# Block 9's burst of attention, block 10's centring and two last stores moved in a fused attention and feed-forward kernel

## The chip, the cores and the metric

The kernel runs on one core of one Trainium2 chip. The metric is device time in microseconds of one execution. A core has five engines with instruction queues of their own: TensorE (PE; matmuls and transposes, its weight loads are listed as PEld), VectorE (DVE), ScalarE (ACT), GpSimd (POOL) and SyncE (SP, which only issues transfers here). The engines run side by side and wait for one another through semaphores; each does its own instructions in the order in which they stand. Transfers are issued from SyncE, ScalarE and GpSimd.

## The reference

Two stages, one behind the other. The first is attention over a sliding window of 128 positions with a linear distance penalty for each head; the second centres and scales each row, runs two dense layers with a ReLU between them, and adds its input.

```python
# q, k, v: 8 batches x 8 heads x 576 positions x 64
scores = scale * np.matmul(q, k.transpose(0, 1, 3, 2))
bias = slopes[:, None, None] * (-np.abs(rel).astype(np.float32))[None, :, :]
mask = (rel >= 0) & (rel < window)
scores = np.where(mask, scores + bias[None], -1000000000.0)
attn = softmax(scores)                  # written out in the reference
x = matmul(attn, v), heads side by side # 8 x 576 x 512

mu, var = mean and variance of each row of x
xn = (x - mu) / np.sqrt(var + 1e-06) * g_ln
out = x + np.maximum(xn @ w_ch1, 0.0) @ w_ch2   # w_ch1 512 x 2048, w_ch2 2048 x 512
```

Inputs and output are float32; the kernel computes with 16-bit floats and sums in float32.

## The kernel before, in words

**Blocks and groups.** The 4608 rows are handled as 36 blocks of 128 rows, in four pairs of batches with nine blocks each (`order`); the ninth block of a pair takes the last 64 positions of both batches. Blocks are gathered into groups for the dense layers: six groups of two blocks (0 to 11), then six of four (`GROUPS`). Groups from `FAST` (6) on do the second layer in another way, with seven products in place of eight (`fast_mlp2`); the change's first part lies before them, its last in the last of them.

**Attention for one block.** Queries and keys are loaded by GpSimd two blocks at a time and turned (`turn`): for the first three pairs of batches TensorE transposes them (L301) into the two score banks (`ps_sc0`, `ps_sc1`), and VectorE copies one bank out and ScalarE the other (L333, L334). The scores of a block (`attend`, L436) go into the same two banks, half of the heads in each; ScalarE takes the exponential (L445) into `probs`, VectorE multiplies it by the mask and decay (L456), and TensorE multiplies by V (L489) into a bank of the pool `ps_mm`. VectorE divides by the sums (L497, L498), which gives `x`.

**Centring.** From block 8 on, `stats` takes mean and variance of `x` on VectorE (L586, L587) and GpSimd makes the reciprocal root of the variance (L541, L544); `normal` then centres and scales on VectorE (L528, into `xc`), and SyncE transposes the result by a transfer (L536) into the group's tile `xT`.

**Dense layers.** `mlp1` has 16 units: four matmuls each (L730) into a bank of `ps_mm`, and one relu, on ScalarE (L746) or for a few units on VectorE (L738). `mlp2` takes each block of the group through four times four matmuls (L763), and `finish` adds `x` on VectorE (L906) and stores. `ps_mm` has four banks, shared by these layers, the products with V and the second layer's sums; a bank is free again when its reader is done.

**What sets the order.** TensorE, VectorE, ScalarE and SyncE have their order written out. `steps` is a list of small pieces of attention work. For each block n from 8 on it has four kinds, here called by letters: A (products with V of block n and scores of block n+2), B (masks of blocks n+1 and n+2, statistics of n), C (a turn further on, where one is due), D (`normal` of block n). `weave_at` runs the units of a dense layer and, behind the units named in its list of places, takes the next pieces from `steps`. The order of GpSimd's instructions (loads, reciprocal roots) isn't written out: a scheduler places them.

In the kernel before, the pieces near the change stand thus: in `mlp1` of group 3, A of block 9 behind unit 13; in its `mlp2`, B9 behind unit 0, C10 (the turn of block 13) and D9 behind unit 1, A10 behind 3, B10 behind 4, D10 behind 5, A11 behind 6; in `mlp1` of group 4, B11 behind unit 0, C12 (the turn of block 15) behind 4, D11 behind 8, A12 and B12 behind 10.

**The last stores.** In the last group, `fast_mlp2` stores the first two blocks whole and the other two by halves of columns: the high half when its sum is ready, the low half, block by block, behind the last product. `store` writes each block in two transfers and gives them in turn to the queues it is told: SyncE and ScalarE. The sums come from VectorE (L847), the stores stand at L921 (the ninth block of a pair) and L925 (the others).

Of the kernel before, what the change touches and what calls it, by code (L numbers as in the profile page):

```python
# [23 lines left out]
NSLOT = 9  # L24
HALF = P // 2
GROUPS = [2] * 6 + [4] * 6
FAST = 6

NV = 10
BY_DMA_TURN = 3  # L30
# [29 lines left out]
def kernel(  # L60
# [10 lines left out]
    nc = tc.nc  # L71
# [548 lines left out]
    for g, size in enumerate(GROUPS):  # L620
        n = sum(GROUPS[:g])
# [3 lines left out]
    count = len(order)  # L625
# [23 lines left out]
    def masks_of(n, *halves):  # L649
        return [(masks,) + order[n] + halves]  # L650

    def warm_step(n):
        return [[(warm, n)]]


    steps = warm_step(11) + [[(turn_first,)]] + warm_step(3)
# [27 lines left out]
    def turn_at(n):  # L684
        ahead = [m for m in (n + 3, n + 4) if m < count and order[m][1] % 2 == 0]
        return [
            f
            for m in ahead
            if by_dma(order[m][0]) == (m == n + 4)
            for f in turn_step(m, True)  # L690
        ]

    steps.append(turn_at(8))
    for n in range(8, count):
        first_half, second_half = values_steps(n)
        step = first_half + second_half[:1]
        if n + 1 < count and order[n + 1][1] == T:
            step += [(scores_tail, order[n][0])]
        if n + 2 < count:
            step += scores_step(n + 2)  # L700
        steps.append(step)
        steps.append(
            [m for t in (n + 1, n + 2) if t < count for m in masks_of(t)] + [(stats, n)]
        )
        if n + 1 < count:
            steps.append(turn_at(n + 1))
        steps.append([(normal, n)])
    combined = combine_w2()
    done = 0

# [10 lines left out]
    def mlp1(g, on_dve=()):  # L721
# [5 lines left out]
        for u, fb in enumerate(turn_about if g >= FAST else range(NFB)):  # L727
# [21 lines left out]
            yield cols  # L749
            if g >= FAST and u == 10:  # L750
                for i in range(4):
                    combine_hidden(g, 0, i)

    def mlp2(g, parts=((0, NFB),)):

        ht = hidden[g]
        sums = {}
        for first, end in parts:
            for at, (p, blk) in enumerate(members[g]):
                if first == 0:  # L760
                    sums[at] = ps_mm.tile([P, DM], FP32, tag="mm", name="ps_m2")
                for fb in range(first, end):
                    nc.tensor.matmul(  # L763
                        sums[at],
                        ht[:, fb, at * P : (at + 1) * P],
                        w2[:, fb, :],
                        start=(fb == 0),
                        stop=(fb == NFB - 1),
                    )
                    if fb % 4 == 3 and fb < NFB - 1:  # L770
                        yield DM
                if end == NFB:
                    finish(p, blk, sums[at])
                    yield DM
# [25 lines left out]
    def fast_mlp2(g):  # L800

        pairs = len(members[g]) // 2
        n0 = sum(GROUPS[:g])
        outs = [out_pool.tile([P, 2, DM], FP32, tag="o", name="o") for _ in range(2)]

        def rows(i):  # L810
            if pairs == 1:
                return x_pairs[n0 // 2][:, i : i + 1, :], outs[0][:, i : i + 1, :]
            return x_pairs[n0 // 2 + i], outs[i]

        x_bank, z_bank, *others = ring
        use = dict(x=[x_bank] * 2, z=[z_bank] * 2)
        use["y"] = use["w"] = others[:1] * 2
        if g == len(GROUPS) - 1:
            use["w"] = others
        ring[:] = others  # L820
        banks = {
            name: [b.rearrange("p (j d) -> p j d", j=2) for b in bs]
            for name, bs in use.items()
        }

        def product(name, lhs, rhs, first):
            for pair in range(pairs):
                for fb in range(QF):
                    nc.tensor.matmul(  # L829
                        banks[name][pair][:, pair, :],  # L830
                        lhs[:, fb, pair * P : (pair + 1) * P],
                        rhs[:, fb, :],
                        start=(
                            first
                            and fb == 0
                            and (pair == 0 or use[name][0] is not use[name][1])
                        ),
                        stop=(fb == QF - 1),
                        skip_group_check=True,
                    )  # L840
                if pair < pairs - 1:
                    yield DM

        def add(name, i, j, to_x, at=slice(0, pairs)):
            x, o = rows(i)
            cols = slice(j * QD, (j + 1) * QD)
            nc.vector.tensor_tensor(  # L847
                out=o[:, at, cols],
                in0=banks[name][at.start][:, at, :],
                in1=(x if to_x else o)[:, at, cols],  # L850
                op=ALU.add,
            )

        def send(i, ats=range(pairs), cols=slice(0, DM), queues=(nc.sync,)):
            _, o = rows(i)
            for at in ats:
                store(*members[g][i * pairs + at], o[:, at, :], cols, queues)

        a = [[hidden_quarter(g, i, j) for j in range(2)] for i in range(2)]
        s = [hidden_sum(g, i) for i in range(4)]  # L860
        combine_hidden(g, 1, 0)
        combine_hidden(g, 1, 1)
        yield from product("x", a[0][0], quarter(0, 0), True)
        add("x", 0, 0, True)
        combine_hidden(g, 1, 2)
        yield DM
        yield from product("y", a[0][1], quarter(1, 0), True)
        add("y", 0, 0, False)
        combine_hidden(g, 1, 3)
        yield DM  # L870
        yield from product("z", s[0], t1, True)
        add("z", 1, 1, True)
        yield DM
        yield from product("x", s[1], t2, False)
        add("x", 0, 1, True)
        yield DM
        yield from product("z", s[3], quarter(1, 1), False)
        add("z", 0, 1, False)
        send(0, queues=(nc.sync, nc.scalar) if g == len(GROUPS) - 1 else (nc.sync,))
        yield DM  # L880
        yield from product("x", s[2], t3, False)
        add("x", 1, 1, False)
        low, high = slice(0, QD), slice(QD, DM)
        if g == len(GROUPS) - 1:
            send(1, cols=high, queues=(nc.sync, nc.scalar))
        add("x", 1, 0, True)
        if use["w"][0] is use["w"][1]:
            yield DM
            ring[:] = [others[1], z_bank, x_bank, others[0]]
            yield from product("w", a[1][1], t4, True)  # L890
            add("w", 1, 0, False)
            send(1)
            yield DM
        else:
            last = product("w", a[1][1], t4, True)
            yield DM
            for at in range(pairs):
                next(last, None)
                add("w", 1, 0, False, slice(at, at + 1))
                send(1, [at], low, (nc.sync, nc.scalar))  # L900
                yield DM
# [27 lines left out]
    def weave_at(units, *places, also=()):  # L929
        for u, _ in enumerate(units):  # L930
            advance_to(done + places.count(u))
            if u in also:
                next(combined, None)
# [13 lines left out]
    with tc.manual_schedule(engines={engine.PE, engine.SP}):  # L947
        with tc.manual_schedule(engines={engine.Activation, engine.DVE}):
            advance_to(first)
            weave_at(mlp1(0, (0, 1)), 2, 7, 8, 9, 13)  # L950
            weave_at(mlp1(1), 2, 8, 12)
            weave_at(mlp2(0, ((0, 8), (8, 12), (12, NFB))), 0, 1, 3, 4, 4, 5)
            weave_at(mlp2(1), 0, 1, 2, 3, 4, 6, 6)
            weave_at(mlp1(2), 0, 3, 3, 6, 8, 11)
            weave_at(mlp2(2), 0, 2, 4, 6, 7)


            weave_at(mlp1(3, (9, 10, 11)), 8, 8, 12, 13)
            weave_at(mlp2(3), 0, 1, 1, 3, 4, 4, 5, 6)
            weave_at(mlp1(4), 0, 4, 8, 10, 10, 14)  # L960
            weave_at(mlp2(4), 0, 2, 2, 5, 5, 7, also=(1, 4, 6))
            weave_at(mlp1(5), 0, 5, 5, 8, 10, 12, also=(3, 6, 9))
            weave_at(mlp2(5), 0, 1, 2, 4, 6, 7)
            ring += [ps_mm.tile([P, DM], FP32, tag="mm", name="ps_r") for _ in range(4)]
            for g in range(6, len(GROUPS)):
                weave_at(
                    mlp1(g), 0, 2, 5, 7, 8, 10, 13, 15, also=(1, 4) if g == 6 else ()
                )
                weave_at(fast_mlp2(g), 1, 3, 6, 7, 7, 10, 12, 13)
# [31 lines left out]
```

## Time and profile before

| what | value |
|---|---|
| median of three runs | 319.14 us (318.6 to 319.21) |
| the profiled execution's own time | 318.21 us |
| its span | 316.4 us |
| mean clock granted to TensorE | 0.996 |
| TensorE busy | 305.0 us, 96% of the span |
| VectorE, ScalarE, GpSimd busy | 228.1, 179.3, 124.9 us |

The span runs from the first to the last instruction of one execution; the rest of the execution's time lies around it. A row of a timeline has start and duration in microseconds, engine, line, operation, output and input tile, shapes, how often it follows itself, and in brackets the idle time of the engine before it and who ended it. SPq and ACTq are the queues from which transfers are issued; the duration of such a row is that of the issue, and the time to landing is given apart. A row of the waits has the waiting engine, tile and line, behind the arrow what it waited for, and then the sum in us, the number of times and the longest. A row of the chain has start, duration and what was done.

### The profile page before, as it was taken

The page shows a single profiled execution, that of the slowest core. Times are in us where ns is not written, and L with a number is a line of the kernel's source. Part 1 is how long each engine was busy: PE and PEld are TensorE (multiplying, and loading weights), DVE is VectorE, ACT ScalarE, POOL GpSimd, SP SyncE. Part 2 cuts the span into 40 slices and gives each one's busy share as a digit, 9 for nine tenths or more (in the row PEclk, how much of TensorE's full clock was granted, in tenths as well). Part 3 has the DMA queues.
Part 4 walks back from the last instruction along what each step waited for, and adds up shares of the span by engine and source line. Part 5 has one row for each costly group of instructions (what it writes and reads, how often), then busy time and mean ns, then how long its engine had stood idle before and what let it go on. Part 6 is the DMA issues. An engine that isn't in the chain of part 4 may idle for free.

```text
span 316.4 us, 9932 instructions
## 1 busy us (share of the span) xinstructions
PE 305.0 (96%) x4195; PEld 205.2 (65%) x4195; DVE 228.1 (72%) x547; ACT 179.3 (57%) x311; POOL 124.9 (39%) x196
## 2 busy tenths in 40 slices
PE   8989999999898999999999999999999999999994
PEld 2468655857657667555885588548855875685483
DVE  2679787877667698768995889479948995761363
ACT  6488765667556658368347832772487247405600
POOL 8923758767155356484345572240001001100000
PEclk9999999999999999999999999999999999999998
DMA  9999999999996999499949994992348044015005
GB/s 111 164 206 199 190 145 184 200 140 149 86 118 79 107 99 157 52 144 68 76 52 158 171 124 53 143 158 52 83 89 132 15 87 86 19 26 125 0 0 136
DMA packets 121183, 34.68 MB, mean 110 GB/s; under 512 B 112049, under 2 KB 116785, under 8 KB 121138
## 3 DMA queue, kind: packets, MB, share of 16 engines
q0 software_dynamic: 89216, 18.36, 71.2%
q1 hardware_dynamic: 31442, 15.15, 25.6%
q8 instruction: 33, 0.54, 0.7%
q10 hardware_dynamic: 480, 0.52, 0.6%
q14 instruction: 12, 0.10, 0.1%
HBM read 36.90 MB, written 9.44 MB: 146 GB/s over the span
## 4 chain that ended last, share of the span: by engine, by line
PE 86%; DVE 6%; ACT 4%; issue 1%; POOL 1%; DVEq 0%; ACTq 0%; POOLq 0%
PE ps_r L730 27%; PE ps_r L829 23%; PE ps_m L763 11%; PE ps_m L730 10%; PE ps_sc L436 5%; PE ps_sc L301 3%; PE ps_r L489 3%; PE ps_pv L489 2%; PE ps_warm L283 2%; ACT probs L445 2%; DVE o L906 1%; DVE x L498 1%; DVE probs L456 1%; DVE o L847 1%; PE ps_tx L581 1%
## 5 line engine op out<-in xcount | busy, mean ns | idle before, releaser
L730 PEld LDWEIGHTS <-w1g 128*128 128x128 f16 x640 | 60.4, 98 | 50.6 <-DVE x L498 1.8
L730 PE MATMUL ps_r<-xT,w1g 128*128 128x512 f16 x384 | 85.1, 379 | 0.0
L445 ACT ACTIVATE probs<-ps_sc 128x1024 f16<-128x1024 f32 x56 | 54.2, 1026 | 51.6 <-PE ps_sc L436 51.5
L746 ACT ACTIVATE ht<-ps_r 128x512 f16<-128x512 f32 x96 | 56.2, 600 | 31.6 <-PE ps_r L730 31.5
L541 POOL TENSOR_TENSOR rstd<-moments,powers 128x1 f32<-128x1 f32 x28 | 6.8, 243 | 102.5 <-DVE moments L587 102.5
L763 PE MATMUL ps_m<-w,ht 128*128 128x512 f16 x192 | 46.0, 380 | 1.2 <-ACT ht L746 1.2
L829 PE MATMUL ps_r<-w,ht 128*128 128x256 f16 x384 | 44.1, 273 | 0.0
L247 POOL DMA_DIRECT2D vx<-in_v_dram x40 | 34.7, 883 | 22.1 <-PE ps_r L489 9.0
L456 DVE TENSOR_TENSOR probs<-probs,m 128x1024 f16<-128x1024 f16 x56 | 37.4, 688 | 7.4 <-ACT probs L445 7.2
L829 PEld LDWEIGHTS <-ht 128*128 128x128 f16 x384 | 37.1, 98 | 4.8
L746 ACT ACTIVATE ht<-ps_m 128x256 f16<-128x256 f32 x91 | 32.9, 391 | 8.5 <-PE ps_m L730 6.2
L730 PE MATMUL ps_m<-xT,w1g 128*128 128x256 f16 x256 | 31.5, 273 | 2.2 <-DVE x L498 0.8
L763 PEld LDWEIGHTS <-ht 128*128 128x128 f16 x192 | 17.1, 98 | 18.8 <-issue 1.3
L237 POOL DMA_DIRECT2D q<-in_q_dram x30 | 20.5, 690 | 17.3 <-PE ps_sc L301 9.3
L586 DVE BATCH_NORM_STATS2 st<-x 128x6 f32<-128x512 f16 x36 | 24.6, 684 | 0.0
L237 POOL DMA_DIRECT2D k<-in_k_dram x30 | 20.2, 687 | 5.8 <-DMA w<-in_moe_w_ch_dram 4.2
L436 PE MATMUL ps_sc<-q,k 64*64 64x128 f16 (+1 forms) x1088 | 20.4, 209 | 1.6 <-ACT probs L445 1.1
L829 PE MATMUL ps_r<-w,hs 128*128 128x256 f16 x192 | 21.9, 273 | 0.0
L489 PEld LDWEIGHTS <-probs 128*128 128x128 f16 x448 | 18.8, 97 | 4.7 <-DVE probs L456 0.3
L829 PEld LDWEIGHTS <-hs 128*128 128x128 f16 x192 | 18.8, 98 | 2.2
L847 DVE TENSOR_TENSOR o<-ps_r,o 128x512 f32<-128x512 f32 (+1 forms) x25 | 16.1, 655 | 5.0 <-PE ps_r L829 4.9
L528 DVE TENSOR_SCALAR xc<-x,moments,rstd 128x512 f16<-128x512 f16 x28 | 12.0, 430 | 10.3 <-POOL rstd L544 10.3
(87 smaller groups left out, 384.3 us busy)
## 6 DMA issues: line engine op xcount, KB each, us to landing
out_dram<-o SPq DMA_DIRECT2D x66, 128.0 KB, 3.1
k<-in_k_dram POOLq DMA_DIRECT2D x32, 128.0 KB, 6.2
vx<-in_v_dram POOLq DMA_DIRECT2D x32, 128.0 KB, 6.7
w<-in_moe_w_ch_dram POOLq DMA_DIRECT2D x8, 512.0 KB, 11.3
q<-in_q_dram POOLq DMA_DIRECT2D x24, 128.0 KB, 4.3
q<-in_q_dram POOLq DMA_DIRECT2D x24, 64.0 KB, 3.8
k<-in_k_dram POOLq DMA_DIRECT2D x8, 64.0 KB, 4.6
vx<-in_v_dram POOLq DMA_DIRECT2D x8, 64.0 KB, 6.4
```

The lines of the kernel that those rows point to most:

```text
L237: nc.gpsimd.dma_start(out=t[b * n // 2 : (b + 1) * n // 2], in_=src[2 * p + b, :, i * P : i * P + n, :].rearrange("h (c r) d -> c h r d", ...
L247: nc.gpsimd.dma_start(out=vx[p0 : p0 + n, :, 0:D], in_=v[b, :, t0 : t0 + n, :].rearrange("h p d -> p h d"),)
L436: nc.tensor.matmul(in_halves(ps[cols, j, n, t, :])[:, r, queries], kt[rows, hp, cols], in_halves(qt[rows, b, hp])[:, r, queries], start=Tr ...
L445: nc.scalar.activation(out=dst.rearrange("p (n j) q -> p j n q", j=2), in_=ps.rearrange("p j n t q -> p j n (t q)"), func=AF.Exp, scale=in ...
L456: nc.vector.tensor_tensor(out=dst, in0=dst, in1=mask, op=ALU.mult)
L489: nc.tensor.matmul(ps[:, i, :], pr[:, h, t, :], vext[(p * NSLOT + o) % NV][:, h, :], start=(n == 0), stop=(n == len(terms) - 1),)
L586: nc.vector.bn_stats(out=st, in_=xs[order[n]])
L730: nc.tensor.matmul(ps[:, 0:cols], w[:, kb, fb * P : (fb + 1) * P], xT[:, kb, 0:cols], start=(kb == 0), stop=(kb == NKB - 1),)
L746: nc.scalar.activation(out=ht[:, fb, 0:cols], in_=ps[:, 0:cols], func=AF.Relu)
L763: nc.tensor.matmul(sums[at], ht[:, fb, at * P : (at + 1) * P], w2[:, fb, :], start=(fb == 0), stop=(fb == NFB - 1),)
L829: nc.tensor.matmul(banks[name][pair][:, pair, :], lhs[:, fb, pair * P : (pair + 1) * P], rhs[:, fb, :], start=(first and fb == 0 and (pair ...
L847: nc.vector.tensor_tensor(out=o[:, at, cols], in0=banks[name][at.start][:, at, :], in1=(x if to_x else o)[:, at, cols], op=ALU.add,)
```

## The change

Three edits.

First, the places of pieces in group 3. In `mlp1(3)` the piece A9 moves from behind unit 13 to behind unit 15, the last. In `mlp2(3)` the seventh piece moves from behind unit 5 to behind unit 6.

Second, the order of pieces around block 11 (`HURRIED`). D10 is no longer put behind C11 but behind A11, and of block 11's own pieces D11 comes ahead of C12. With the unchanged places of group 4, that gives: A11 and D10 behind unit 6 of `mlp2(3)`; B11 behind unit 0 of `mlp1(4)`, D11 behind unit 4, C12 behind unit 8, A12 and B12 behind unit 10 as before.

Third, `send` cycles through its queues over all the blocks it stores, where each block began anew before, and the high halves of the last two blocks go to SyncE, GpSimd, GpSimd and ScalarE in that order, where they went to SyncE, ScalarE, SyncE and ScalarE. The two low halves still begin anew, SyncE and then ScalarE, for each block.

No amount of work changes. On GpSimd the scheduler sets another order near the change: both issues of block 20's keys stand ahead of the second step (L544) of block 9's reciprocal root, where one did, the first of them now ahead of its first step (L541) too, and the load of V into buffer 9 stands ahead of block 10's reciprocal root, where it stood behind it. Line numbers behind the edits move by two or three.

```diff
-FAST = 6
+FAST, HURRIED = 6, 11
...
-        steps.append(
-            [m for t in (n + 1, n + 2) if t < count for m in masks_of(t)] + [(stats, n)]
-        )
-        if n + 1 < count:
-            steps.append(turn_at(n + 1))
-        steps.append([(normal, n)])
+        to_mask = [m for t in (n + 1, n + 2) if t < count for m in masks_of(t)]
+        turns = [turn_at(n + 1)] if n + 1 < count else []
+        if n == HURRIED:
+            steps += [[(normal, n - 1)], to_mask + [(stats, n)], [(normal, n)], *turns]
+        else:
+            steps += [to_mask + [(stats, n)], *turns]
+            if n != HURRIED - 1:
+                steps.append([(normal, n)])
...
         def send(i, ats=range(pairs), cols=slice(0, DM), queues=(nc.sync,)):
             _, o = rows(i)
+            queues = cycle(queues)
             for at in ats:
                 store(*members[g][i * pairs + at], o[:, at, :], cols, queues)
...
-            send(1, cols=high, queues=(nc.sync, nc.scalar))
+            send(1, cols=high, queues=(nc.sync, nc.gpsimd, nc.gpsimd, nc.scalar))
...
-            weave_at(mlp1(3, (9, 10, 11)), 8, 8, 12, 13)
-            weave_at(mlp2(3), 0, 1, 1, 3, 4, 4, 5, 6)
+            weave_at(mlp1(3, (9, 10, 11)), 8, 8, 12, 15)
+            weave_at(mlp2(3), 0, 1, 1, 3, 4, 4, 6, 6)
```

## The prediction

> **What bounds the kernel now.** I read the page's busy time first, then the list of TensorE's waits by stretch, then the timelines of each engine where a wait stands.
>
> ```profile
> span 316.4 us, 9932 instructions
> PE 305.0 (96%) x4195; PEld 205.2 (65%) x4195; DVE 228.1 (72%) x547; ACT 179.3 (57%) x311; POOL 124.9 (39%) x196
> ```
>
> TensorE is busy for 96% of the span, so only the holes in TensorE's work, and what follows its last product, can be won. Between 75 and 120 us, where the change reorders, its waits are these:
>
> ```profile
> PE ps_m L763 <- ACT ht L746: 1.2, 1, 1.2
> PE ps_m L730 <- DVE x L498: 0.8, 1, 0.8
> PE ps_m L730 <- DMA xT<-xc: 0.4, 1, 0.4
> PE ps_m L730 <- DVE o L906: 0.4, 1, 0.4
> ```
>
> The first three sit where the change acts; the last (at 116.4) lies behind it. No later wait on a transfer is listed, so what is won here has nothing further on that must swallow it, other than waits which move along with TensorE.
>
> **Step 1: block 9's burst** (block 9's products with V, block 11's scores) **from behind unit 13 of group 3's first layer to behind unit 15, its last.**
>
> ```profile
> 81.58 0.42 PE L489 MATMUL ps_pv<-vx,own 128*128 128x65 f16 x8
> 81.94 0.58 PE L436 MATMUL ps_sc<-q,k 64*64 64x128 f16 x32
> 82.45 1.05 PE L730 MATMUL ps_m<-xT,w1g 128*128 128x256 f16 x8
> 84.67 1.89 PE L763 MATMUL ps_m<-w,ht 128*128 128x512 f16 x8 [1.17 <-ACT ht L746]
> 86.49 0.45 PE L301 MATMUL ps_sc<-iden,q 64*64 64x64 f16 x32
> ...
> 82.41 1.94 ACT L445 ACTIVATE probs<-ps_sc 128x1024 f16<-128x1024 f32 x2 [0.24 <-PE ps_sc L436]
> ```
>
> Today units 14 and 15 (82.45) follow the burst; their relus stand on ScalarE behind the two exponentials (82.41 for 1.94 us), and the second layer's first product at 84.67 needs the bank that unit 14's relu frees. One unit takes 0.45 us (six from 99.11 to 101.82, rows in step 3), so the units end at 82.45 + 0.90 = 83.35 and the hole is 1.32 us. Moved, units 14 and 15 run at 81.58, their relus precede the exponentials, the burst follows at 82.48 (scores at 82.84), and the product starts at 83.35.
>
> What is late next: block 13's transposes (86.49 now) write the banks of block 11's scores. The exponentials start 0.47 us behind their scores (81.94 to 82.41), so at 83.31, and end at 85.25; the transposes' own place is 83.35 + 1.82 (84.67 to 86.49) = 85.17. They wait about 0.1 us and start near 85.26, **1.23 us** earlier.
>
> That does not all arrive, because the order of GpSimd moves too: the reciprocal root of block 9's variance (L544) now stands behind both of block 20's key loads, before behind one.
>
> ```profile
> 87.26 1.43 POOL L237 DMA_DIRECT2D q<-in_q_dram  x2 [6.92 <-PE ps_sc L301]
> 88.82 0.70 POOL L237 DMA_DIRECT2D k<-in_k_dram  x1
> 89.53 0.58 POOL L544 TENSOR_TENSOR rstd<-rstd,powers 128x1 f32<-128x1 f32 x1
> 90.06 0.77 POOL L237 DMA_DIRECT2D k<-in_k_dram  x1
> ...
> 90.15 0.41 DVE L528 TENSOR_SCALAR xc<-x,moments,rstd 128x512 f16<-128x512 f16 x1 [1.81 <-POOL rstd L544]
> 95.28 0.41 DVE L528 TENSOR_SCALAR xc<-x,moments,rstd 128x512 f16<-128x512 f16 x1 [0.94 <-POOL rstd L544]
> 95.61 0.17 DVE L497 RECIPROCAL rec<-ps_pv 128x4 f32<-128x4 f32 x1
> 96.36 0.42 DVE L498 SCALAR_TENSOR_TENSOR x<-ps_pv,rec 128x256 f16<-128x256 f32 x1
> 96.71 0.74 DVE L906 SCALAR_TENSOR_TENSOR o<-ps_m,rstd,x 128x512 f32<-128x512 f32 x1
> ...
> 90.59 1.20 SPq L536 DMA_TRANSPOSE xT<-xc  x1
> ...
> 97.50 0.60 PE ps_m L730 x4
> ```
>
> The loads start when the transposes have read the raw tiles, and VectorE stands in block 9's centring (90.15) until the root is there, with the second layer's result, block 10's values and masks queued behind it. One more load issue costs 0.70 to 0.77 us. The centring thus moves by 1.23 - 0.70 = **0.53 us** only.
>
> **Step 2: block 10's centring behind block 11's products.** VectorE now waits 0.94 us in it (95.28) for its root; block 11's values (95.61 to 96.78, 1.17 us) and the second layer's last result (96.71) are behind, and TensorE at 97.50 needs that result's bank. Behind the values, the root's 0.94 us run beside 1.17 us of work: the wait goes. One load of V moves ahead of this root on GpSimd; it waits for block 11's products, which then lie over 2 us ahead of the root's statistics, so I cost it at nothing; without that cover it would cost up to 0.94 us, the wait taken away. The order on SyncE stays. TensorE's unit 3 of group 4 starts at 97.50 - 0.53 - 0.94 = 96.03, **1.47 us** earlier. Its other input, block 9's transposed tile, comes 0.53 us earlier than the product at 94.86 below: 94.33, and 3 units later it is 95.69, so VectorE decides. That hole at group 4's first unit grows, from 0.4 to about 1.2 us; the holes behind it shrink.
>
> **Step 3: block 11's centring ahead of block 15's turn, the turn from behind unit 4 of group 4 to behind unit 8.** The turn's 64 transposes pass 16 products; its two copies on ScalarE pass four relus and come near the exponentials of block 14.
>
> ```profile
> 94.86 0.60 PE L730 MATMUL ps_m<-xT,w1g 128*128 128x256 f16 x4 [0.38 <-DMA xT<-xc]
> 98.46 0.45 PE L301 MATMUL ps_sc<-iden,q 64*64 64x64 f16 x32
> 99.11 2.88 PE L730 MATMUL ps_m<-xT,w1g 128*128 128x256 f16 x24
> 101.82 0.65 PE L489 MATMUL ps_pv<-vx,probs 128*128 128x65 f16 x16
> 102.40 0.63 PE L436 MATMUL ps_sc<-q,k 64*64 64x128 f16 x32
> 102.96 1.92 PE L730 MATMUL ps_m<-xT,w1g 128*128 128x256 f16 x16
> 105.13 0.60 PE L730 MATMUL ps_m<-xT,w1g 128*128 128x256 f16 x4 [0.25 <-ACT ht L746]
> ...
> 99.43 0.59 ACT L333 COPY q<-ps_sc 128x512 f16<-128x512 f16 x1 [0.47 <-PE ps_sc L301]
> 99.91 0.74 ACT L334 COPY k<-ps_sc 128x512 f16<-128x512 f16 x1
> ```
>
> From 96.03: six units (2.71) to the turn at 98.74, 0.65 for it, two units, products with V (0.58): block 14's scores could start at 100.87. ScalarE's copies end 2.19 us behind the turn's start (98.46 to 100.65), at 100.93: 0.1 us of wait. Scores 0.56, unit 11 at 101.54. ScalarE does two relus (0.3 each) behind the copies and then 1.94 us of exponentials, from 101.55 to 103.49, then unit 11's relu (0.38): unit 15 at 103.91 where 105.13 stands now, that is **-1.22 us**. So step 3 gives back 0.25. GpSimd's loads that wait for this turn start some 0.3 us later than now; they feed a block seven further on, and I cost them at nothing. Block 11's centring stands at most 0.94 us in VectorE, with only the turn's copies behind it, and TensorE's six units cover it.
>
> **Step 4: two of the last block pair's stores on GpSimd.** High halves: one store less on each of SyncE and ScalarE, two on GpSimd.
>
> ```profile
> 311.78 0.78 DVE L847 TENSOR_TENSOR o<-ps_r,o 128x256 f32<-128x256 f32 x2
> 311.65 0.87 ACTq L921 DMA_DIRECT2D out_dram<-o  x1
> 312.61 0.57 ACTq L925 DMA_DIRECT2D out_dram<-o  x1
> 313.27 0.55 ACTq L921 DMA_DIRECT2D out_dram<-o  x1
> 312.95 0.54 SPq L921 DMA_DIRECT2D out_dram<-o  x1
> ...
> DMA to landing us min/median/max: 2.0/2.0/2.1
> DMA to landing us min/median/max: 2.6/4.6/6.6
> DMA to landing us min/median/max: 2.4/4.0/7.1
> ```
>
> (The three landings: the L921 stores, GpSimd's L234 loads, the xT transposes.) VectorE is done at 312.56; the last store issues at 313.27 because ScalarE's queue was held to 312.52 by the store at 311.65. With one store less its last comes near 312.95, as SyncE's does, so the last landing moves from 315.3 to 315.0: **-0.3 us**, and no more, since SyncE's last stays. GpSimd issues at about 311.1 and 311.8 (0.70 each); no store of its is in the trace. Its nearest rows, the L234 loads, land in 2.6 to 6.6 us: 314.4 to 318.4. I take the low end, because nothing else loads then, while those loads are issued several in a row and convert types.
>
> [...] The row's median of 4.6 would give 316.4, a loss of 1.1 us in place of that gain. [...]
>
> **Sum.** -1.2 - 0.3 = -1.5 us. The profiled execution took 318.21 us (316.4 of span and 1.8 around it) and becomes 316.7. The median of the three runs, 319.14, lies 0.9 above it; from that, **317.6 us**.
>
> **Rivals.**
> - *The transposed tile comes late.* Block 9's transpose took some 4.2 us (issued at 90.59, TensorE goes on at 94.86); landings run from 2.4 to 7.1. Up to 4.5 us it costs nothing; beyond, it delays unit 3 one for one. At 5.3 the reordering gives -0.4 (with the tail 318.4), at 7.1 +1.1 (320.0). Against it: the second key load now precedes the transpose by a microsecond, where before it was issued beside it.
> - *The gain is given back.* The wait at 116.4 us on VectorE, or ScalarE's burst in step 3 (two copies, two relus, two exponentials, 3.8 us for 2.3 us of TensorE's work), takes another microsecond. Then some -0.3 is left: 318.8, no change. For it: the banks turn over four at a time there; against: what feeds VectorE comes earlier too.
> - *The store on GpSimd is the last to land: slower.* It costs from a landing of 3.2 us on, cancels everything at 4.7, and at 6.6 the end is 3.1 us later: -1.2 + 3.1 = +1.9, 321.0. For it: the median of 4.6; against: that median's crowd.
> - *The change does nothing in the tail*, SyncE's last store deciding: 317.9. It is within the forecast.
>
> **Chances.** The forecast 0.58 (317.0 to 318.2), the late tile 0.12, the gain given back 0.14, the late store 0.16. A difference under 0.2%, 0.6 us, about what a measurement here can tell from none, comes from the given-back gain and from part of the stores that land in 4 to 5 us. Faster 0.71, same 0.15, slower 0.14. The range goes from 316.5 (the tile early, no wait in step 3) to 319.3, which leaves out the late landings.
>
> **What would show it.** Right: the wait of L763 on ScalarE gone; GpSimd's root near 89.0 behind two key loads; block 10's centring without a wait; group 4's first unit with a wait on xT of about 1 us and unit 3 near 96.0; unit 15 near 103.9, the rest shifted by 1.2 us; the last issue near 312.95 less the shift. Wrong: a landing over 3.2 us on GpSimd's stores, or a new TensorE wait over 1 us between 98 and 117.

## The result, and the profile after

The changed kernel takes 317.56 us, median of 8 executions (316.86 to 317.95), against 318.70 (318.06 to 319.21, also 8) for the kernel before on the same chip: a ratio of 0.9962, with a 95% interval of 0.9949 to 0.9976. By the ratio that is 1.2 us less (0.8 to 1.6), by the medians 1.1. The prediction was 317.6. Its -1.5 us was taken from a median of three runs, 319.14, that lay 0.4 above the one measured beside the result.

The profiled execution took 317.64 us, 315.8 of it span. First the page's busy time of the kernel after, then TensorE's waits between 75 and 120 us.

```profile
span 315.8 us, 9932 instructions
PE 304.8 (97%) x4195; PEld 205.2 (65%) x4195; DVE 228.8 (72%) x547; ACT 179.7 (57%) x311; POOL 125.8 (40%) x198
```

```profile
PE ps_m L732 <- DVE o L909: 0.7, 2, 0.4
PE ps_m L732 <- DVE x L498: 0.6, 1, 0.6
PE ps_m L732 <- ACT ht L748: 0.2, 1, 0.2
```

The busy time is the same, the holes are smaller: 1.5 us of waits in place of 2.8. The 1.2 us on ScalarE's relu (L763 before, L765 now) are gone, and so is the wait for the transposed tile; what is left are three short waits on VectorE and one on ScalarE.

Spans of single executions don't show a change of this size by themselves. The profile after is 0.69 us late before it comes to anything that was moved, so I measure from a mark that lies ahead of the change: the start of VectorE's three relus in group 3's first layer, 80.04 us before and 80.73 after (next two fences, the timelines of VectorE of before and of after).

```profile
80.04 1.30 DVE L738 TENSOR_SCALAR ht<-ps_m 128x256 f16<-128x256 f32 x3 [1.67 <-PE ps_m L730]
```

```profile
80.73 1.30 DVE L740 TENSOR_SCALAR ht<-ps_m 128x256 f16<-128x256 f32 x3 [1.67 <-PE ps_m L732]
...
310.75 0.78 DVE L849 TENSOR_TENSOR o<-ps_r,o 128x256 f32<-128x256 f32 x2
```

From the mark to the start of VectorE's last two additions (311.78 before, 310.75 after) I call the **stretch**, from there to the end of the span the **tail**, which is known to 0.05 us, since the span is given to 0.1. The stretch went from 231.74 to 230.02 us, -1.72; the tail from 4.62 to 5.05, +0.43. So the reordering gave more than the -1.2 forecast, and the edit of the stores, costed at -0.3, takes time.

TensorE's timeline after, at the places of the prediction's steps:

```profile
83.15 0.42 PE L489 MATMUL ps_pv<-vx,own 128*128 128x65 f16 x8
83.50 0.58 PE L436 MATMUL ps_sc<-q,k 64*64 64x128 f16 x32
84.02 1.90 PE L765 MATMUL ps_m<-w,ht 128*128 128x512 f16 x8
85.96 0.45 PE L301 MATMUL ps_sc<-iden,q 64*64 64x64 f16 x32
...
92.91 1.04 PE L765 MATMUL ps_m<-w,ht 128*128 128x512 f16 x4
93.83 0.60 PE L732 MATMUL ps_m<-xT,w1g 128*128 128x256 f16 x4
95.05 1.16 PE L732 MATMUL ps_m<-xT,w1g 128*128 128x256 f16 x8 [0.63 <-DVE x L498]
96.58 2.78 PE L732 MATMUL ps_m<-xT,w1g 128*128 128x256 f16 x24 [0.37 <-DVE o L909]
99.29 0.45 PE L301 MATMUL ps_sc<-iden,q 64*64 64x64 f16 x32
...
104.13 0.60 PE L732 MATMUL ps_m<-xT,w1g 128*128 128x256 f16 x4 [0.25 <-ACT ht L748]
```

The second layer (84.02) starts straight behind the burst. Counted from the mark, block 13's transposes (85.96) come 1.22 us earlier than before, unit 3 of group 4 (96.58) 1.61 and unit 15 (104.13) 1.69. The same on VectorE and on GpSimd:

```profile
90.28 0.41 DVE L528 TENSOR_SCALAR xc<-x,moments,rstd 128x512 f16<-128x512 f16 x1 [1.89 <-POOL rstd L544]
...
94.92 0.17 DVE L497 RECIPROCAL rec<-ps_pv 128x4 f32<-128x4 f32 x1
95.12 0.42 DVE L498 SCALAR_TENSOR_TENSOR x<-ps_pv,rec 128x256 f16<-128x256 f32 x1
95.46 0.40 DVE L528 TENSOR_SCALAR xc<-x,moments,rstd 128x512 f16<-128x512 f16 x1
```

```profile
88.12 0.70 POOL L237 DMA_DIRECT2D k<-in_k_dram  x1
88.82 0.22 POOL L541 TENSOR_TENSOR rstd<-moments,powers 128x1 f32<-128x1 f32 x1
88.95 0.71 POOL L237 DMA_DIRECT2D k<-in_k_dram  x1
89.66 0.59 POOL L544 TENSOR_TENSOR rstd<-rstd,powers 128x1 f32<-128x1 f32 x1
```

GpSimd's root (89.66) stands behind both key loads, and VectorE still waits 1.89 us for it in block 9's centring, which, counted from the mark, comes 0.56 us earlier than before. Block 10's centring (95.46) has no wait.

### The profile page after: what moved, and what is told of

It reads as the page before. It is cut to its first block, busy times and chain, and to the rows that moved or that the text cites. A ratio compares the mean times of both kernels' runs of the same rounds, so it can differ in the third digit from the quotient of the medians.

```text
span 315.8 us, 9932 instructions
## 1 busy us (share of the span) xinstructions
PE 304.8 (97%) x4195; PEld 205.2 (65%) x4195; DVE 228.8 (72%) x547; ACT 179.7 (57%) x311; POOL 125.8 (40%) x198
## 4 chain that ended last, share of the span: by engine, by line
PE 84%; DVE 6%; ACT 4%; issue 2%; DMA 1%; POOL 1%; DVEq 0%; ACTq 0%
PE ps_r L732 27%; PE ps_r L831 23%; PE ps_m L732 10%; PE ps_m L765 9%; PE ps_sc L436 4%; PE ps_sc L301 3%; PE ps_r L489 3%; PE ps_warm L283 2%; PE ps_pv L489 2%; ACT probs L445 2%; DMA q<-in_q_dram 1%; DVE x L498 1%; DVE o L909 1%; DVE probs L456 1%; DVE o L849 1%
## 5 line engine op out<-in xcount | busy, mean ns | idle before, releaser
L541 POOL TENSOR_TENSOR rstd<-moments,powers 128x1 f32<-128x1 f32 x28 | 6.9, 245 | 99.1 <-DVE moments L587 98.1
L765 PE MATMUL ps_m<-w,ht 128*128 128x512 f16 x192 | 46.0, 380 | 0.0
L765 PEld LDWEIGHTS <-ht 128*128 128x128 f16 x192 | 17.0, 98 | 17.5
```

What stands on the lines that cost most here:

```text
L765: nc.tensor.matmul(sums[at], ht[:, fb, at * P : (at + 1) * P], w2[:, fb, :], start=(fb == 0), stop=(fb == NFB - 1),)
```

## The experiments

The table has each kernel's profiled stretch and tail, the median of its executions and its ratio to the kernel before as it ran beside it (318.50 us beside e1 to e4, 318.38 beside e5 to e8, 318.13 beside e9 to e11).

| kernel | stretch | tail | median us | ratio, 95% interval |
|---|---|---|---|---|
| before | 231.74 | 4.62 | 318.70 | 1 |
| after | 230.02 | 5.05 | 317.56 | 0.9962 [0.9949, 0.9976] |
| e1, reordering alone | 230.06 | 4.69 | 316.81 | 0.9940 [0.9920, 0.9959] |
| e2, stores alone | 231.63 | 5.05 | 318.61 | 0.9999 [0.9986, 1.0013] |
| e3, burst alone | 232.47 | 4.67 | 318.28 | 0.9986 [0.9966, 1.0007] |
| e4, centring alone | 230.62 | 4.67 | 317.42 | 0.9959 [0.9941, 0.9978] |
| e5, e1 with the turn first | 230.16 | 4.62 | 316.71 | 0.9948 [0.9929, 0.9967] |
| e6, e1 with statistics first | 229.57 | 4.59 | 315.94 | 0.9922 [0.9902, 0.9942] |
| e7, after without GpSimd's stores | 230.06 | 4.93 | 316.96 | 0.9954 [0.9937, 0.9971] |
| e8, after with one GpSimd store | 230.04 | 4.62 | 316.74 | 0.9944 [0.9925, 0.9963] |
| e9, e6 with the key loads later | 229.19 | 4.69 | 315.23 | 0.9910 [0.9897, 0.9922] |
| e10, e3 with statistics first | 229.76 | 4.62 | 316.56 | 0.9952 [0.9938, 0.9965] |
| e11, e3 once more | 230.69 | 4.63 | 318.69 | one execution |

### e1 and e2: the reordering and the stores, apart

e1 is the kernel after with the stores as before; e2 is the kernel before with the stores as after.

```diff
 # e1, against after
-            queues = cycle(queues)
...
-            send(1, cols=high, queues=(nc.sync, nc.gpsimd, nc.gpsimd, nc.scalar))
+            send(1, cols=high, queues=(nc.sync, nc.scalar))
```

> The two edits of the order without the third: all last stores on SyncE and ScalarE as before. Two stretches are read: from VectorE's first relu of group 3 (80.04 us before, 80.73 after) to the start of its last pair of adds (311.78 and 310.75), which is 231.74 us before and 230.02 after; and from there to the span's end, 4.62 before and 5.05 after. Theory A (the reordering wins 1.7 us, more than the 1.2 predicted, and the stores on GpSimd cost 0.4): stretch 230.0, end 4.6, time 1.7 us under the kernel before. Theory B (the prediction: 1.2 won by the order, 0.3 by the stores): stretch 230.5, end 4.6, time 1.2 us under. Theory C (the stores do nothing, the difference of the ends is chance): the time of the changed kernel, 1.1 us under.

> The third edit alone: two of the last stores on GpSimd, the order as before. Stretch 231.7 us under all theories. Theory A: end 5.05 us, time 0.4 us over the kernel before. Theory B: end 4.3 us, time 0.3 us under. Theory C: end between 4.5 and 5.1 by chance, time unchanged.

The two effects are separate and add up. e1 has the stretch of after and the tail of before; e2 has the stretch of before (231.63) and the tail of after (5.05). The reordering is worth -1.7 us, by the traces (231.74 to 230.06) and by the medians (318.5 to 316.81). The stores' edit costs 0.4 us of tail in both kernels that have it, too little for the timed runs of e2 alone to show it. Both stretches and both tails are those of Theory A.

### e3 and e4: the burst and the centring, apart

```diff
 # e3, against before
-            weave_at(mlp1(3, (9, 10, 11)), 8, 8, 12, 13)
+            weave_at(mlp1(3, (9, 10, 11)), 8, 8, 12, 15)
```

e4 is e1 with the burst back behind unit 13.

> The first place alone: block 9's burst behind unit 15 of group 3's first layer, centring and stores as before. By the prediction's step 1 the hole at the second layer goes (1.2 us at the transposes), but the root of block 9 still stands behind both key loads, so that VectorE's chain moves by 0.5 only and unit 3 of group 4 with it: stretch 231.2 us, time 0.5 us under. Rival: the hole closed counts in full, 230.5 us and 1.2 us under.

> Block 10's centring behind block 11's products and block 11's ahead of the turn, the burst and the stores as before. By the prediction's step 2 the wait of 0.94 us in block 10's centring goes, and the hole of 1.2 us ahead of the second layer stays: stretch 230.8 us, time 0.9 us under. Rival: only with the burst moved does it help, since GpSimd's load of V now stands ahead of the root: 231.7 us, no change.

The centring alone has -1.12 us of stretch, near the -0.9 expected, with no wait in block 10's centring and the hole of 1.17 us ahead of the second layer still there. With the burst moved as well (e1) the stretch is another 0.56 shorter, near the 0.53 at which the prediction's step 1 arrives. The burst alone makes the stretch 0.73 us *longer*, which neither expectation allows for, although block 9's centring comes 0.55 us earlier, as in the kernel after. TensorE's timeline of e3 and the views of two windows show why:

```profile
93.71 0.60 PE L730 MATMUL ps_m<-xT,w1g 128*128 128x256 f16 x4
96.38 3.59 PE L730 MATMUL ps_m<-xT,w1g 128*128 128x256 f16 x16 [2.07 <-DVE x L498]
...
93.00:96.50 3.50, 1.43 (x9) 0.71 (x8) 2.45 (x8) 2.00 (x3) 1.36 (x3) 0.99 0.95 117
96.50:100.00 3.50, 3.50 (x28) 2.22 (x30) 3.01 (x6) 1.15 (x3) 0.19 (x1) 0.52 0.57 113
```

(A row of a window has its start and end, its length, the busy time of TensorE and then of the others, and behind these the granted TensorE clock, here 0.99 and 0.52.) Group 4's first unit runs at 93.71, and then TensorE waits 2.07 us for block 11's values, which stand on VectorE behind block 10's centring and its 0.94 us wait. The 16 products behind this hole take 3.59 us, and the granted clock is 0.52 in the row that holds nearly all of them. The 12 timed executions of e3 fall in two clusters: six of 317.1 to 317.8 us with a mean granted clock of 0.996 to 1.000, six of 318.8 to 319.5 us with 0.992 to 0.995. The median of the first six, 317.4, is 1.1 under the kernel before. e10 and e11 follow this up.

### e11 and e10: is it the hole that costs the clock?

e11 is e3 once more, for a second trace. e10 is e3 with block 9's statistics ahead of the masks, which brings VectorE earlier.

```diff
 # e10, against e3
+        to_mask = [m for t in (n + 1, n + 2) if t < count for m in masks_of(t)]
+        steps.append([(stats, n)] + to_mask if n == 9 else to_mask + [(stats, n)])
```

> The burst alone once more, for a second trace of the same program. Theory: the idle time of 2.07 us at block 11's values is there in every execution, and whether the clock falls behind it changes from one to the next; if this one has a full clock, the 16 products behind the idle time take 2.2 us instead of 3.6 and the stretch is near 231.0 instead of 232.47. Rival: the executions with full clock have a shorter idle time (under 1.3 us, as the kernel before has).

> The burst alone, with the statistics of block 9 ahead of the masks, so that VectorE comes 1.35 us earlier to block 10's centring and its wait there stays. Theory: the burst alone loses TensorE's clock because TensorE idles 2.07 us at block 11's values (granted clock 0.52 in the 3.5 us behind it in the profile; of its 12 executions the six that took 318.8 to 319.5 us had a mean clock of 0.992 to 0.995, the six that took 317.1 to 317.8 one of 0.996 to 1.000). With VectorE earlier no idle time is over 1 us there, the clock stays full (0.996 or more in all executions), and the time is near 316.4 us in one cluster. Rival: the clock falls for another reason (the place of the burst, or the share of busy time over a longer stretch): again about half of the executions at 0.992 to 0.995, some 1.7 us longer.

e11's timeline and windows have the same hole with the clock intact:

```profile
97.20 2.03 PE L730 MATMUL ps_m<-xT,w1g 128*128 128x256 f16 x16 [2.08 <-DVE x L498]
...
93.00:96.30 3.30, 2.12 (x49) 1.19 (x44) 2.32 (x6) 2.22 (x3) 1.67 (x3) 1.00 1.04 143
96.30:100.00 3.70, 2.80 (x82) 2.19 (x83) 3.63 (x9) 1.54 (x4) 0.00 (x0) 1.00 0.52 74
```

The hole is 2.08 us, the 16 products take 2.03, and the stretch is 230.69: the clock costs e3's trace 1.78 us of stretch, 1.56 of it in these products, and with a full clock the burst alone is worth -1.05, between the two expectations for e3 (-0.5 and -1.2). (e11's one time of 318.69 says nothing on that, since its mark was already 1.4 us later than that of before, at 81.48.) In e10 the longest hole there is 0.73 us,

```profile
94.56 2.65 PE L729 MATMUL ps_m<-xT,w1g 128*128 128x256 f16 x20 [0.73 <-DVE rec L497]
```

all five executions have a clock of 0.997 or more, and they lie in one cluster, 316.53 to 316.94. So with the hole of 2.1 us the clock falls in one trace of two, and six of the 13 executions of this program have the lower mean clock. With shorter holes that is rare: of the 50 executions of the kernel before (in its trace, behind the program's start, waits up to 1.2 us) that ran beside the experiments one had a mean clock under 0.996 (0.992, 319.67 us), and of e7's ten one (0.994, 317.87 us). No trace shows what idled TensorE in these two.

What decides between the two outcomes is not shown: the hole is 2.07 us in e3's trace and 2.08 in e11's.

### e5: the turn back ahead of block 11's centring

```diff
 # e5, against e1
-            steps += [[(normal, n - 1)], to_mask + [(stats, n)], [(normal, n)], *turns]
+            steps += [[(normal, n - 1)], to_mask + [(stats, n)], *turns, [(normal, n)]]
```

> The reordering without the stores' edit, and with block 15's turn back behind unit 4 of group 4 and block 11's centring behind unit 8. The prediction's step 3 said that the later turn gives back 0.25 us, because ScalarE's two copies come near block 14's exponentials: by it this kernel is 0.25 us faster than the reordering alone (stretch 229.8 against 230.06). Rival, from the trace after, where the copies end ahead of the exponentials with room: the place of the turn costs nothing, stretch within 0.1 of 230.06. Second rival: with its values behind it, the centring behind the turn's copies on VectorE comes later and costs, stretch 230.3 or more.

Stretch 230.16 against 230.06: the place of the turn costs nothing. The prediction's +0.25 for it isn't there.

### e6: block 9's statistics ahead of the masks

```diff
 # e6, against e1
-            steps += [to_mask + [(stats, n)], *turns]
+            steps += [[(stats, n)] + to_mask if n == 9 else to_mask + [(stats, n)], *turns]
```

> The reordering without the stores' edit, and the statistics of block 9 on VectorE ahead of the masks that stand before them. GpSimd's root of block 9 then stands between the query loads and ahead of both key loads. If those loads in front of the root are what the wait of block 9's centring is made of, the centring comes about 1.4 us earlier (mark + 8.2), and VectorE, which runs on without a wait from there to block 11's values, hands these over earlier: TensorE's waits on x (0.5 us) and on the second layer's result (0.4) go, stretch 229.1, time 0.9 us below the reordering alone. Rival: the masks, 0.9 us later, hold up the products that follow, which gives back as much: stretch 230.0 to 230.9. Second rival: the root waits for the statistics and not for the loads: centring and stretch unchanged.

GpSimd's timeline of e6, and then TensorE's:

```profile
85.74 0.74 POOL L237 DMA_DIRECT2D q<-in_q_dram  x1 [5.06 <-PE ps_sc L301]
86.50 0.21 POOL L541 TENSOR_TENSOR rstd<-moments,powers 128x1 f32<-128x1 f32 x1
86.63 0.70 POOL L237 DMA_DIRECT2D q<-in_q_dram  x1
87.34 0.58 POOL L544 TENSOR_TENSOR rstd<-rstd,powers 128x1 f32<-128x1 f32 x1
87.87 1.45 POOL L237 DMA_DIRECT2D k<-in_k_dram  x2
```

```profile
91.92 1.03 PE L765 MATMUL ps_m<-w,ht 128*128 128x512 f16 x4
93.67 4.09 PE L732 MATMUL ps_m<-xT,w1g 128*128 128x256 f16 x36 [0.71 <-DVE xc L528]
```

With the root ahead of the key loads, block 9's centring comes 8.21 us behind the mark instead of 9.56, 1.35 us earlier: the two key loads in front of the root are what held it. It still waits 1.14 us for the root, which stands behind the query loads. The two waits on VectorE at group 4 are gone as well, but the stretch gains only 0.49 us, because a wait of 0.71 stands ahead of group 4's first product. The profile puts it down to VectorE's centring of block 10, which that product doesn't need. What it needs is block 9's transposed tile, issued at 88.39, and its landing, quoted below, is 5.1 us later, at 93.5.

### e9: the key loads behind the transpose

Block 20's key loads are held back by a small memset of VectorE into their raw tile, behind block 10's values. The edit also writes the other loads of queries and keys for blocks 17 to 20 at that point, but holds none of them: from the mark to the transpose GpSimd's work stands as in e6, without the key loads.

```diff
 # e9, against e6
+EARLY = [[tag, *at] for at in ((1, 4), (2, 0), (2, 1)) for tag in "qk"]
...
+        if held:
+            nc.vector.memset(t[:, 0, 0, 0:2], 0.0)
...
+        if n == 10:
+            step = step + [(load_early,)]
```

> As with the statistics first, and both key loads of block 20 held back until VectorE has block 10's values (a memset of two columns of the raw tile, 0.1 us, stands there ahead of them), some 1.6 us behind the issue of block 9's transpose instead of around it. Theory: the transpose lands late (5.1 us with the statistics first, 3.0 in the kernel after, 4.1 before) because the key loads are issued beside it; ahead of them it lands in 3 us or less, TensorE's wait of 0.7 us at group 4's first product goes, stretch 228.9 against 229.57. Rival: the transpose is late for another reason (the stores behind it on SyncE, its own 1.2 us of issue): landing 5 us, stretch 229.6. Second rival: the loads, now later, delay something behind (block 10's root on GpSimd, the loads' own reader): the wait goes and another of that size comes, stretch 229.6.

The tile's landing, from the view of tile xT around block 9's transpose alone. In before:

```profile
DMA to landing us min/median/max: 4.1/4.1/4.1
```

In after:

```profile
DMA to landing us min/median/max: 3.0/3.0/3.0
```

In e6:

```profile
DMA to landing us min/median/max: 5.1/5.1/5.1
```

In e9:

```profile
DMA to landing us min/median/max: 2.6/2.6/2.6
```

And GpSimd's and TensorE's timelines of e9:

```profile
91.06 1.39 POOL L240 DMA_DIRECT2D k<-in_k_dram  x2 [2.76 <-issue]
...
93.17 4.25 PE L742 MATMUL ps_m<-xT,w1g 128*128 128x256 f16 x36
```

The second key load was issued 1.7 us ahead of the transpose in after (88.95 and 90.66), 0.5 us ahead in before (90.06 and 90.59), 0.2 us behind it in e6, and over 2 us behind in e9. The transpose took 3.0, 4.1, 5.1 and 2.6 us. Beside the loads it is late; clear of them, on either side, it isn't. The other traces agree: 2.8 to 3.1 us in the six with GpSimd's order of after, 3.8 and 3.9 in e4 and e2 with that of before, 5.2 in e10 with that of e6. With the loads later the wait of 0.7 us goes, and unit 15 comes 0.85 us earlier than in e6, but of that only 0.38 reaches the end of the stretch: at 123.20 us TensorE waits for a relu of ScalarE, where e6 has no wait, and from there on e9 is 0.37 us ahead. e9 has the lowest median of the study, 315.23 us, 0.9910 [0.9897, 0.9922] of before; the interval of e6 reaches down to 0.9902.

### e7 and e8: where the stores' time goes

```diff
 # e7, against after: both loops of store()
-                next(queues).dma_start(out=dst, in_=src)
+                eng = next(queues)
+                if eng is not nc.gpsimd:
+                    eng.dma_start(out=dst, in_=src)
 # e8, against after
-            send(1, cols=high, queues=(nc.sync, nc.gpsimd, nc.gpsimd, nc.scalar))
+            send(1, cols=high, queues=(nc.sync, nc.gpsimd, nc.sync, nc.scalar))
```

> The kernel after with the two stores on GpSimd left out, so that the high column half of two quarters of the last four blocks is not written. SyncE and ScalarE have what they have after. First theory: GpSimd's stores themselves, by their transfers or GpSimd's drain, cost the 0.4 us: from the start of the last pair of adds to the end 4.3 to 4.6 us instead of 5.05, and from the last landing to the end 1.1 instead of 1.6. Second theory: the last landing is one that SyncE's closing list of waits asks for early, and the rest of the list comes behind it: 5.0 and 1.6, as with the stores.

> The kernel after with the high halves on SyncE, GpSimd, SyncE and ScalarE: one store on GpSimd instead of two. First theory (GpSimd's stores themselves cost, each its share or one as much as two): from the start of the last pair of adds to the end 4.85 to 5.05 us, and 1.4 to 1.6 from the last landing to the end. Second theory (the place of the last landing in SyncE's closing list): the last landings move one place down the list, 1.1 to 1.3 from the last landing to the end, 4.4 to 4.7 in all.

First the kernel after: the last store on ScalarE's queue, and GpSimd's own two stores in the list of transfers. Then the last two issues of e8.

```profile
311.80 0.78 ACTq L924 DMA_DIRECT2D out_dram<-o  x1
...
out_dram<-o POOLq DMA_DIRECT2D x2, 64.0 KB, 2.3
```

```profile
311.23 0.56 ACTq L924 DMA_DIRECT2D out_dram<-o  x1
311.46 0.59 SPq L924 DMA_DIRECT2D out_dram<-o  x1
```

GpSimd's stores are no trouble: they start at 310.34 and 310.93 and land 2.3 us after issue, ahead of the last ones of the other queues. They aren't what ends last. SyncE's closing waits for the stores (us in total, number, longest), in before:

```profile
SPq L996 <- DMA out_dram<-o: 1.5, 3, 0.6
```

In after:

```profile
SPq L999 <- DMA out_dram<-o: 1.7, 2, 1.2
```

In e7:

```profile
SPq L1003 <- DMA out_dram<-o: 1.6, 2, 1.1
```

In e8:

```profile
SPq L999 <- DMA out_dram<-o: 1.0, 4, 0.4
```

SyncE ends the program: it waits for the transfers one completion after another, in the same order in the traces of before and after, and then closes. From the trace's records of landings and of these waits, in us from the end of VectorE's last addition:

| kernel | last issue | last landing | its place in SyncE's order | end of the span | landing to end |
|---|---|---|---|---|---|
| before | 0.71, ScalarE | 2.73 | fifth | 3.87 | 1.14 |
| e1 | 0.70, ScalarE | 2.72 | fifth | 3.86 | 1.15 |
| after | 0.27, ScalarE | 2.64 | third | 4.24 | 1.61 |
| e2 | 0.27, ScalarE | 2.69 | third | 4.30 | 1.61 |
| e7 | 0.27, ScalarE | 2.54 | third | 4.15 | 1.61 |
| e8 | 0.50, SyncE | 2.58 | fifth | 3.85 | 1.27 |

After and e7 wait long for two transfers and pass the others, before and e8 wait for three and four. The edit does bring the last issue 0.44 us forward, but that store's issue lengthens (0.78 us against 0.55) and its landing moves by 0.1 us only. Behind the landing SyncE still has to go through the rest of its order. In after, e2 and e7 that holds two more waits, 0.16 us, and a pause of 0.37 us between two of them. The pause is in e8 too, but ahead of its wait for the last landing, which ends 0.15 us behind that landing. In all four it stands ahead of the 208th of SyncE's records in the trace; after, e2 and e7 have one issue on SyncE less than before and e8, so that it comes one wait later in the order. In before the 208th record is the wait for the last landing itself, and it ends with the landing.

e7, with no store on GpSimd at all, keeps after's 1.61; e8, with one, has 1.27 and the tail of before, as the second theory has it for both. So the cost isn't that of GpSimd's stores; it goes with what SyncE has left to do when the last transfer lands, the pause included. What the pause is, no run shows.

The longer issue goes with a neighbour: in after, e2 and e7 SyncE issues its last store 0.04 us ahead of ScalarE's. In e8 ScalarE's same store is issued at the same 0.27 us, but SyncE's comes 0.23 us behind it; the issue takes 0.56 us, and the landing follows it by 2.07 us instead of 2.37. Why two issues so close cost more stays open; a pair earlier in the tail of after that starts within 0.01 us of each other takes 0.47 and 0.50 us.

## Why the prediction was right, and where it was not

**Step 1** held term by term: the hole on ScalarE's relu gone, block 13's transposes 1.22 us earlier against 1.23, block 9's centring 0.56 earlier against 0.53, because GpSimd's root stands behind one load more. e6 shows that this is the reason: with the root ahead of both, the centring comes 1.35 us earlier. On top of the centring's move (e4 to e1) the burst is worth 0.56 us. What step 1 left out is that without step 2 the earlier start of group 4 opens a hole of 2.07 us, behind which TensorE's granted clock was 0.52 in e3's trace and 1.00 in e11's.

**Step 2** held in its size, not in its detail. Block 10's wait of 0.94 went, and unit 3 came 1.61 us earlier against 1.47; of the 0.14 more, 0.12 is VectorE doing the same work from block 9's centring to the second layer's last result in 5.50 us (90.28 to 95.78) where it took 5.62 without its wait (90.15 to 96.71, less 0.94). The sub-claim that failed is "That hole at group 4's first unit grows, from 0.4 to about 1.2 us": there is no wait on the tile at all (93.83 starts straight behind 92.91). I had taken over the 4.2 us that the transpose needed before; it needed 3.0, since the loads were issued further ahead of it. I had written down just that as the reason against the late tile, and didn't put it into the sum. It changed no total, as VectorE decided there anyway, with 0.63 and 0.37 us of waits.

**Step 3** failed: "So step 3 gives back 0.25" has no counterpart. Unit 15 is at -1.69, unit 3 at -1.61. ScalarE's timeline after shows the term that was oversized:

```profile
100.11 0.59 ACT L333 COPY q<-ps_sc 128x512 f16<-128x512 f16 x1 [0.34 <-PE ps_sc L301]
100.60 0.74 ACT L334 COPY k<-ps_sc 128x512 f16<-128x512 f16 x1
101.19 0.67 ACT L748 ACTIVATE ht<-ps_m 128x256 f16<-128x256 f32 x2
101.86 1.94 ACT L445 ACTIVATE probs<-ps_sc 128x1024 f16<-128x1024 f32 x2
103.69 1.50 ACT L748 ACTIVATE ht<-ps_m 128x256 f16<-128x256 f32 x5
```

In these rows an instruction starts before the row in front of it has ended: 0.59 us after a copy of 0.74, 1.83 after exponentials of 1.94. The sum took the relu behind the turn's copies from the copies' end, 2.19 us behind the turn's start; here it starts 1.90 us behind it (99.29 to 101.19). From unit 3 to the exponentials it is 5.28 us (96.58 to 101.86), where the sum had 5.52. (Two additions of that sum are also 0.04 to 0.05 high: 100.93 and 0.56 make 101.49, 103.49 and 0.38 make 103.87.) e5, with the turn back at its old place, confirms that the place costs nothing.

**Step 4** failed in sign: -0.3 forecast, +0.4 measured, in after and in e2. "With one store less its last comes near 312.95" was right in kind (0.44 us earlier relative to VectorE's end), and the low end taken for GpSimd's landing, 2.6, was close to the 2.3 measured. Wrong was "the last landing moves from 315.3 to 315.0": it moved by 0.1, and the end of the program isn't the last landing but SyncE's closing behind it, 1.14 us before and 1.61 after, a term that the sum takes as unchanged.

**The total** is near by luck: the reordering gave 0.5 us more than its -1.2, the stores took 0.7 more than their -0.3, and the median of before that the sum was set against lay 0.4 high, which made up for the rest. The mechanism of the reordering was right, that of the stores wrong. Two of the rivals' sums are loose as well: a microsecond given back leaves -0.5 of -1.5, not -0.3, and a landing at 7.1 us, 2.6 over 4.5, makes +1.4 of -1.2, with the stores' -0.3 then 320.2. Of the rivals, the gain given back and the late store on GpSimd didn't come. The late tile didn't come in this kernel, but e6 and e10 have it, with a landing of 5.1 to 5.2 us; its mechanism was right. The tail that gives nothing was the nearest to the truth and still too kind.

## What to carry to other kernels

Price a reordering by what then waits next on each engine: here one edit alone opened a hole of 2.07 us, behind which the granted clock was 0.52 in one of two traces, and the other closed it. For a transfer that decides, look at what other queues issue around it: here holding two key loads back let a transpose land in 2.6 us instead of 5.1, of which 0.4 us reached the end of the stretch. At the end of a program look at what follows the last landing: here what SyncE still had to go through took 1.14 to 1.61 us, while the last issue 0.44 us earlier moved the landing by 0.1.

## What the runs showed of the hardware that was not expected

- A hole of 2.07 us in TensorE's work was followed by a granted clock of 0.52 over 3.5 us (96.5 to 100 in e3), at a cost of 1.78 us of stretch against e11, where the same program with the same hole (2.08 us) kept 1.00.
- A transpose by transfer of one block took 2.6 to 5.2 us to land: 3.0 with the second key load issued on GpSimd 1.7 us ahead of it, 4.1 with 0.5 us, 5.1 with that load 0.2 us behind it, 2.6 with it over 2 us behind.
- From the last landing to the end of the span it took 1.14 to 1.15, 1.27 or 1.61 us, by how many of SyncE's waits, and whether a pause of 0.37 us among them, came behind it.
